# The opening of a fused attention and mixture kernel: the first pair's queries turned in two parts, the second pair's keys turned at once

## The chip, the cores and the metric

The kernel runs on one core of a Trainium2 chip, as one program. The metric is the device time of one execution in microseconds. Three runs of the kernel before took 676.3, 675.15 and 675.15 us; the median is 675.15.

## What is computed

The reference has three parts, and each feeds the next. Only the first matters for the change.

```
B, H, S, D = 4, 8, 576, 64
def rotate(x):                       # by position, halves of D
    x1, x2 = x[..., :32], x[..., 32:]
    return concat([x1*cos - x2*sin, x1*sin + x2*cos])
scores = matmul(rotate(q), rotate(k).T) / sqrt(D)
attn = exp(scores - max(scores));  attn /= sum(attn) + 1e-9
x = matmul(attn, v)                  # 4 x 8 heads of 576 x 64
```

After it come a gated layer with a mixing product over the 576 positions, and four causal attention experts of which each position takes two. All values are float32.

## The kernel before

**Tiling.** The attention goes through the 32 heads as 16 pairs. The two heads of a pair stand one above the other, 64 rows each, in tiles of 128 rows by 576 columns (positions). Queries and keys are loaded together with a copy whose halves are swapped, so that turning (the rotation by position) is three elementwise operations on the whole tile: two multiplications by tables (`rp`) and one sum. Head 1 of a pair has its positions rotated by 64 columns.

**Splitting.** TensorE multiplies at reduced precision, so each turned operand is split: a high part, rounded to `F32R`, and a low part, the remainder. A score tile is a sum of a product of stacked high and low queries (tile `q2`, 128 rows: one head's high part in one half, its low part in the other) with the keys' high part repeated in both halves (`kh`), and a product of the high queries (`qz`, the other half zero) with the keys' low part (`kl`).

**Two ways to fill these operands.** For the first pair of all, `Work.first` (L386 to 416) writes them by engine instructions: ScalarE copies with rounding, VectorE subtracts, GpSimd makes the low parts of columns 256 to 575. For every other pair, `Work.parts` (L426 to 440) makes a high tile `hi` and a low tile `lo`, and `fill_k` (L149) and `fill_q` (L158) spread them by transfers on SyncE's queue: four for the keys, four for the queries (the high part of head 0, its low part, the high part of head 1, its low part).

**The blocks.** A pair has nine score tiles: two heads by four blocks of 128 queries, and one tile of the last 64 of both heads. `slot(k)` (L538) issues one step of the pipeline; with n = k // 9 the pair and x = k % 9 the block, it issues in this order: the exponential of block x (ScalarE), the score products of the next block (TensorE, `scores`), the transposes of the block before (`turn`), the maximum of the next block (VectorE, `maxima`, called the block's maximum here), pending sums of the next pair's turning, the copies of the transposed block, the products with the values, and the preparation of the next pairs. Score tiles alternate between two pairs of banks, so block x + 2 waits for the exponential of block x.

**What sets the order.** All of this is in one program order: `tc.keep_in_program_order` holds for every instruction of an engine (L57 to 61), so each engine runs its own instructions in the order in which the text issues them. A transfer on SyncE's queue that waits holds up those behind it.

**The opening.** L657 to 670 issue what stands ahead of the blocks: 40 products of zeros (`warmed`, two TensorE instructions each), the loads of the first pair in the order keys, tables, queries, constants, values, `first`, the loads of the second pair (keys, then queries), the two multiplications of its keys on GpSimd, its values, the loads of the third pair, the two multiplications of its queries on GpSimd, and then the first score tile and its maximum. Buffers for loaded queries and keys are two deep, so the third pair's loads reuse the first pair's tiles and wait for their last reader. The sums of the second pair follow on VectorE in blocks 2 (keys) and 3 (queries), its parts in blocks 3 (keys) and 4 (queries):

```
            if n == 0 and x in (2, 3):
                works[1].rope(3 - x, (2,), DVE)
...
                if x == (4 if n == 0 else 1):
                    nx.parts(0, DVE if n else ACT)
                if x == (2 if n else 3):
                    nx.parts(1, DVE if n else ACT)
```

Behind each of the first four blocks stand two more zero products (L676). The functions:

Of the kernel before, what the change touches and what calls it, by code (L numbers as in the profile page):

```python
# [12 lines left out]
ALU = mybir.AluOpType  # L13
AX = mybir.AxisListType

B, H, S, D = 4, 8, 576, 64
# [28 lines left out]
def fused_kernel(ctx, tc, qk, v, w_in, w_out, w_sg, g_ln, b_sg, wqk, wvg, wo, rope, cst, out):  # L45
# [68 lines left out]
    class Pair:  # L114
# [43 lines left out]
        def fill_q(self, qh, ql, part=(0, 1)):  # L158
            q2, qz = self.q2, self.qz
            a, c = slice(0, 64), slice(64, 128)  # L160
            todo = [(q2[a, 0, 0:S], qh[a, :]), (qz[a, 0], qh[a, :]), (q2[c, 0, 0:S], ql[a, :])]
            if self.turned:
                def twice(h, o, z, i):
                    o, z, i = f(o), f(z), f(i)
                    o = bass.AP(tensor=o.tensor, offset=o.offset, ap=[o.ap[0], [z.offset - o.offset, 2], [1, S]])
                    return o, bass.AP(tensor=i.tensor, offset=i.offset, ap=[i.ap[0], [0, 2], [1, S]])

                todo = [twice(a, q2[a, 0, 0:S], qz[a, 0], qh[a, :]), (q2[c, 0, 0:S], ql[a, :]),
                        twice(c, q2[c, 1, 64:640], qz[c, 1], qh[c, :]), (q2[a, 1, 64:640], ql[c, :])]
                todo = [x for i, x in enumerate(todo) if i % 2 in part]  # L170
            else:
                todo += [(q2[c, 1, 0:512], qh[c, 0:512]), (qz[c, 1, 64:S], qh[c, 0:512]), (q2[a, 1, 0:512], ql[c, 0:512])]
            if not self.turned:
# [159 lines left out]
    with ExitStack() as st:  # L333
# [30 lines left out]
        class Work:  # L364
# [21 lines left out]
            def first(self):  # L386
# [6 lines left out]
                def low(o, x, h, engine=DVE):  # L393
                    engine.tensor_tensor(o, x, f(h), op=ALU.subtract)

                for t in (k, q):
                    for i in range(2):
                        DVE.tensor_tensor(t[:, i], t[:, i], rp[:, i], op=ALU.mult)
                    DVE.tensor_tensor(t[:, 0], t[:, 0], t[:, 1], op=ALU.add)
                q, k, s, s1 = q[:, 0], k[:, 0], slice(0, S), slice(64, 640)  # L400
                ACT.copy(kh[a, 0], k[a])
                ACT.copy(kh[c, 0], k[a])
                ACT.copy(kh[c, 1], k[c])
                hi = one.tile([P, S], F32R, tag="hi1", name="hi1")
                DVE.tensor_copy(hi, k)
                low(kl, k, hi)
                ACT.copy(kh[a, 1], k[c])
                ACT.copy(q2[a, 0, s], q[a])
                ACT.copy(qz[a, 0], q[a])
                ACT.copy(qz[c, 1], q[c])  # L410
                u, w = slice(0, 256), slice(256, S)
                low(q2[c, 0, u], q[a, u], q2[a, 0, u])
                DVE.tensor_copy(q2[c, 1, s1], q[c])
                low(q2[a, 1, 64:320], q[c, u], q2[c, 1, 64:320])
                low(q2[a, 1, 320:640], q[c, w], q2[c, 1, 320:640], POOL)
                low(q2[c, 0, w], q[a, w], q2[a, 0, w], POOL)

            def rope(self, x, steps=(0, 1, 2), engine=POOL):
                t = self.ts[x]
# [118 lines left out]
        def slot(k):  # L538
# [5 lines left out]

            if w:
                w.exps(x)
            if x == 0 and p:
                p.out(False)
            if x == 4 and p:
# [22 lines left out]
            if x == 0 and p:  # L572
                p.factor(0)

            if n == 0 and x in (2, 3):
                works[1].rope(3 - x, (2,), DVE)
            if wk and not (nx and x == 5):
                if late:
                    wk.place(4)
# [72 lines left out]
        def warmed(n):  # L652

            for _ in range(n):
                PE.matmul(warm[:, 0:P], zero, zero, start=True, stop=True)

        fixed[0] = True  # L657
        warmed(40)
        works[0].load(0)
        works[0].load_values()  # L660
        works[0].first()
        works[1].load(1)
        works[1].rope(1, (0, 1))
        works[1].load_values()
        works[2] = Work()
        works[2].load(2)
        works[1].rope(0, (0, 1))
        works[0].start()
        works[0].scores(0)
        works[0].maxima(0)  # L670
# [2 lines left out]
        for k in range(9 * B * NP + 7):  # L673
            n, x = divmod(k, 9)
            slot(k)
            if k < 4:  # L676
                warmed(2)
            if x in W_AT[4 if n == NP * B - 1 else min(n, 2 + n % 2)]:
# [871 lines left out]
```

## Time and profile before

| | |
|---|---|
| median of three runs | 675.15 us (675.15 to 676.3) |
| profiled execution | 674.28 us, span 672.5 us |
| TensorE busy | 662.9 us, 99% of the span |
| VectorE, ScalarE, GpSimd busy | 446.6, 433.6, 342.3 us |
| granted TensorE clock, mean | 1.000 |

The span is the time from the first to the last instruction of the profiled execution. PE is TensorE, PEld its weight load, DVE VectorE, ACT ScalarE, POOL GpSimd, SPq the queue of SyncE that issues transfers. All engine instructions go through one helper, so the rows carry L59 for nearly everything, and are told apart by their tiles: `ps_S` is a score tile, `ps_t` a transposed one, `ps_l` takes the zero products and small transposes, `ps_o` the products with the values; `t` is the loaded and turned tile, `hi` and `lo` its parts, `q` the operand tile of the queries, `nmax` the maxima, `e` the exponentials. In a timeline, instructions of one kind that follow one another are merged into one row with their count. Ends of TensorE's products are modelled.

### The profile page before, as it was taken

The numbers are of one execution on the slowest core, as the hardware profiler recorded it, in microseconds if no ns is written. First come the engines' busy times: TensorE is split into PE (matmuls) and PEld (weight loads), VectorE is DVE, ScalarE is ACT, GpSimd is POOL, SyncE is SP. The second block draws the span as 40 slices with busy tenths as digits, with TensorE's granted clock in tenths as the row PEclk, the third lists the DMA queues.
The fourth block names the chain that finished last, engine by engine and source line by source line (L and its number), as shares of the span: only waits on it lengthen the run. The fifth ranks groups of instructions, "written<-read, shape, count | busy, mean of one in ns | idle before, by whom it ended". The sixth has DMA issues, their size and how long they took to land.

```text
span 672.5 us, 13535 instructions
## 1 busy us (share of the span) xinstructions
PE 662.9 (99%) x4741; PEld 585.5 (87%) x4741; DVE 446.6 (66%) x1011; ACT 433.6 (64%) x1033; POOL 342.3 (51%) x333
## 2 busy tenths in 40 slices
PE   8999999999999999999999999999999999999997
PEld 8777777777777777798999999999999999999885
DVE  5877777767777776578964764664247666656674
ACT  6777777877878777673563473472146776666774
POOL 2877788888888832642456127206212451542320
PEclk9999999999999999999999999999999999999999
DMA  7798888887888852661374243055466364553522
GB/s 270 209 283 269 249 237 248 242 239 241 228 254 227 249 150 90 182 189 34 118 222 143 89 134 115 12 142 161 121 182 150 92 171 96 135 160 76 143 82 79
DMA packets 64449, 112.83 MB, mean 168 GB/s; under 512 B 18991, under 2 KB 24190, under 8 KB 64382
## 3 DMA queue, kind: packets, MB, share of 16 engines
q1 hardware_dynamic: 61646, 106.29, 54.8%
q10 hardware_dynamic: 2736, 5.68, 2.8%
q8 instruction: 38, 0.62, 0.4%
q14 instruction: 29, 0.24, 0.1%
HBM read 58.06 MB, written 18.98 MB: 115 GB/s over the span
## 4 chain that ended last, share of the span: by engine, by line
PE 87%; DVE 4%; DMA 3%; ACT 2%; issue 1%; POOL 1%; SPq 1%; POOLq 0%; ACTq 0%; DVEq 0%
PE ps_S L59 46%; PE ps_o L59 16%; PE ps_t L59 13%; PE ps_f L59 5%; PE ps_l L59 3%; PE ps_s L59 3%; DMA ws<-in_w_sg_dram 1%; DMA mask<-in_cst_dram 1%; DVE ga L59 1%; DMA q<-lo 0%; DVE nmax L59 0%; DVE t L59 0%; DMA r<-d 0%; DMA sr<-rd 0%; ACT vh L59 0%
## 5 line engine op out<-in xcount | busy, mean ns | idle before, releaser
L59 DVE TENSOR_REDUCE nmax<-ps_S 128x1 f32<-128x576 f32 x144 | 108.8, 756 | 54.3 <-PE ps_S L59 51.6
L59 ACT ACTIVATE e<-ps_S,nmax 128x576 f32<-128x576 f32 x144 | 107.9, 749 | 34.2 <-DVE nmax L59 32.6
L59 PE MATMUL ps_t<-ident,e 128*128 128x128 f32 x776 | 118.1, 273 | 0.0
L59 PEld LDWEIGHTS ps_t<-ident,e 128*128 128x128 f32 x776 | 94.2, 140 | 3.7 <-ACT wih L59 0.4
L59 PE MATMUL ps_S<-kh,q 128*128 128x288 f32 x352 | 84.9, 333 | 2.6 <-ACT e L59 1.4
L59 POOL TENSOR_TENSOR t<-t,rp 128x576 f32<-128x576 f32 x60 | 84.6, 1431 | 0.1
L59 PEld LDWEIGHTS ps_S<-kh,q 128*128 128x128 f32 x352 | 52.2, 189 | 28.8 <-issue 12.8
L59 PE MATMUL ps_o<-g,v 128*64 128x320 f32 (+1 forms) x512 | 72.7, 415 | 0.0
L59 ACT COPY g<-ps_t 128x512 f32<-128x512 f32 x95 | 55.6, 586 | 23.3 <-PE ps_t L59 23.2
L59 POOL TENSOR_TENSOR lo<-t,hi 128x576 fp32r<-128x576 f32 x30 | 43.1, 1438 | 43.6 <-DVE hi L59 42.2
L59 PE MATMUL ps_S<-lo,q 128*128 128x288 f32 x304 | 65.2, 295 | 0.0
L59 PEld LDWEIGHTS ps_o<-g,v 128*64 128x64 f32 x512 | 32.4, 136 | 24.3 <-issue 4.9
L59 PE MATMUL ps_S<-yh,w 128*128 128x288 f32 x256 | 51.8, 304 | 0.0
L59 POOL TENSOR_TENSOR yl<-x,yh 128x640 fp32r<-128x640 f32 (+1 forms) x16 | 25.0, 1564 | 51.6 <-ACT yh L59 51.5
L59 ACT ACTIVATE e<-e,nmax 128x128 f32<-128x128 f32 (+4 forms) x72 | 42.3, 588 | 13.6 <-DVE nmax L59 13.5
L59 PEld LDWEIGHTS ps_S<-lo,q 128*128 128x128 f32 x304 | 48.6, 188 | 0.0
L59 POOL TENSOR_TENSOR t<-t 128x576 f32<-128x576 f32 x28 | 39.7, 1418 | 2.2
L59 ACT ACTIVATE ga<-ga 128x512 f32<-128x512 f32 (+1 forms) x34 | 22.3, 656 | 26.9 <-DVE ga L59 26.9
L59 PEld LDWEIGHTS ps_S<-yh,w 128*128 128x128 f32 x256 | 38.7, 189 | 0.1
L59 POOL TENSOR_TENSOR xl<-sa,xh 128x576 fp32r<-128x576 f32 x12 | 17.7, 1484 | 40.9 <-ACT xh L59 34.7
L59 DVE CUSTOM_DVE_ANT_0 e<-ps_s,mask 128x128 f32<-128x128 f32 (+3 forms) x64 | 31.0, 486 | 7.9 <-PE ps_s L59 6.0
L59 POOL TENSOR_TENSOR gxl<-u,gxh 128x576 fp32r<-128x576 f32 x16 | 22.8, 1429 | 25.3 <-ACT gxh L59 25.3
(283 smaller groups left out, 1758.5 us busy)
## 6 DMA issues: line engine op xcount, KB each, us to landing
t<-in_qk_dram SPq DMA_DIRECT2D x32, 576.0 KB
kh<-hi SPq DMA_DIRECT2D x92, 144.0 KB
q<-hi SPq DMA_DIRECT2D x30, 288.0 KB
q<-lo SPq DMA_DIRECT2D x38, 144.0 KB
v<-in_v_dram SPq DMA_DIRECT2D x16, 320.0 KB
sa<-xr SPq DMA_DIRECT2D x16, 288.0 KB
xd<-sa SPq DMA_DIRECT2D x16, 288.0 KB
xr<-xd SPq DMA_DIRECT2D x16, 288.0 KB
```

Of the source, the lines that this page charges most:

```text
L59: ins = op(*a, **k)
```

## The change

In `first`, the queries' turning is cut at column 320. The function becomes a generator of five steps: the keys and the queries' columns 0 to 319 are turned; then all copies and low parts that these allow, with the queries' copies of head 0 ahead of the second head's keys; behind block 0 the queries' columns 320 to 575 are turned on VectorE; in block 1 their copies and low parts follow (both low parts on GpSimd); in block 2 ScalarE's last copy. The opening has 24 zero products instead of 40. The multiplications of the second pair's keys keep their place in the text, but GpSimd has nothing of `first` ahead of them any more; those of its queries move into block 1, behind the low parts of the first pair's second columns. The sum of the second pair's queries moves from block 3 to block 4. In `fill_q`, when all four transfers are issued together (this is so for the second pair alone), both high parts go ahead of both low parts.

```diff
--- before.py
+++ after.py
@@ -167,7 +167,7 @@
 
                 todo = [twice(a, q2[a, 0, 0:S], qz[a, 0], qh[a, :]), (q2[c, 0, 0:S], ql[a, :]),
                         twice(c, q2[c, 1, 64:640], qz[c, 1], qh[c, :]), (q2[a, 1, 64:640], ql[c, :])]
-                todo = [x for i, x in enumerate(todo) if i % 2 in part]
+                todo = [x for h in part for x in todo[h::2]]
             else:
                 todo += [(q2[c, 1, 0:512], qh[c, 0:512]), (qz[c, 1, 64:S], qh[c, 0:512]), (q2[a, 1, 0:512], ql[c, 0:512])]
             if not self.turned:
@@ -393,27 +393,40 @@
                 def low(o, x, h, engine=DVE):
                     engine.tensor_tensor(o, x, f(h), op=ALU.subtract)
 
-                for t in (k, q):
+                def turn(t, s):
                     for i in range(2):
-                        DVE.tensor_tensor(t[:, i], t[:, i], rp[:, i], op=ALU.mult)
-                    DVE.tensor_tensor(t[:, 0], t[:, 0], t[:, 1], op=ALU.add)
-                q, k, s, s1 = q[:, 0], k[:, 0], slice(0, S), slice(64, 640)
+                        DVE.tensor_tensor(t[:, i, s], t[:, i, s], rp[:, i, s], op=ALU.mult)
+                    DVE.tensor_tensor(t[:, 0, s], t[:, 0, s], t[:, 1, s], op=ALU.add)
+
+                u, w = slice(0, 320), slice(320, S)
+                turn(k, slice(0, S))
+                turn(q, u)
+                yield
+                t, q, k = q, q[:, 0], k[:, 0]
                 ACT.copy(kh[a, 0], k[a])
                 ACT.copy(kh[c, 0], k[a])
+                ACT.copy(q2[a, 0, u], q[a, u])
+                ACT.copy(qz[a, 0, u], q[a, u])
                 ACT.copy(kh[c, 1], k[c])
+                ACT.copy(kh[a, 1], k[c])
+                ACT.copy(qz[c, 1, u], q[c, u])
                 hi = one.tile([P, S], F32R, tag="hi1", name="hi1")
                 DVE.tensor_copy(hi, k)
                 low(kl, k, hi)
-                ACT.copy(kh[a, 1], k[c])
-                ACT.copy(q2[a, 0, s], q[a])
-                ACT.copy(qz[a, 0], q[a])
-                ACT.copy(qz[c, 1], q[c])
-                u, w = slice(0, 256), slice(256, S)
                 low(q2[c, 0, u], q[a, u], q2[a, 0, u])
-                DVE.tensor_copy(q2[c, 1, s1], q[c])
-                low(q2[a, 1, 64:320], q[c, u], q2[c, 1, 64:320])
-                low(q2[a, 1, 320:640], q[c, w], q2[c, 1, 320:640], POOL)
+                DVE.tensor_copy(q2[c, 1, 64:384], q[c, u])
+                low(q2[a, 1, 64:384], q[c, u], q2[c, 1, 64:384])
+                yield
+                turn(t, w)
+                yield
+                ACT.copy(q2[a, 0, w], q[a, w])
+                ACT.copy(qz[a, 0, w], q[a, w])
                 low(q2[c, 0, w], q[a, w], q2[a, 0, w], POOL)
+                DVE.tensor_copy(q2[c, 1, 384:640], q[c, w])
+                low(q2[a, 1, 384:640], q[c, w], q2[c, 1, 384:640], POOL)
+                yield
+                ACT.copy(qz[c, 1, w], q[c, w])
+                yield
 
             def rope(self, x, steps=(0, 1, 2), engine=POOL):
                 t = self.ts[x]
@@ -544,6 +557,10 @@
 
             if w:
                 w.exps(x)
+            if k in (1, 2):
+                next(first)
+            if k == 1:
+                works[1].rope(0, (0, 1))
             if x == 0 and p:
                 p.out(False)
             if x == 4 and p:
@@ -572,8 +589,8 @@
             if x == 0 and p:
                 p.factor(0)
 
-            if n == 0 and x in (2, 3):
-                works[1].rope(3 - x, (2,), DVE)
+            if n == 0 and x in (2, 4):
+                works[1].rope(int(x == 2), (2,), DVE)
             if wk and not (nx and x == 5):
                 if late:
                     wk.place(4)
@@ -655,16 +672,17 @@
                 PE.matmul(warm[:, 0:P], zero, zero, start=True, stop=True)
 
         fixed[0] = True
-        warmed(40)
+        warmed(24)
         works[0].load(0)
         works[0].load_values()
-        works[0].first()
+        first = works[0].first()
+        next(first)
+        next(first)
         works[1].load(1)
         works[1].rope(1, (0, 1))
         works[1].load_values()
         works[2] = Work()
         works[2].load(2)
-        works[1].rope(0, (0, 1))
         works[0].start()
         works[0].scores(0)
         works[0].maxima(0)
@@ -673,6 +691,8 @@
         for k in range(9 * B * NP + 7):
             n, x = divmod(k, 9)
             slot(k)
+            if k == 0:
+                next(first)
             if k < 4:
                 warmed(2)
             if x in W_AT[4 if n == NP * B - 1 else min(n, 2 + n % 2)]:
```

## Rows read from the trace of the kernel before

**Rows 1.** Busy by stretch: us; PE, PEld, DVE, ACT, POOL; clock, DMA share, GB/s
```profile
12.80:30.00 17.20, 14.96 (x116) 12.95 (x115) 12.77 (x20) 12.18 (x29) 15.55 (x12) 1.00 0.65 174
25.00:30.00 5.00, 4.18 (x32) 3.60 (x31) 3.69 (x6) 3.76 (x11) 4.92 (x4) 1.00 0.97 243
30.00:120.00 90.00, 90.00 (x677) 69.67 (x677) 66.08 (x135) 68.84 (x178) 70.07 (x51) 1.00 0.88 260
```

**Rows 2.** Chain of waits, 0 to 60: start us, us, what
```profile
1.04 12.01 PE ps_l L59 x80
...
20.72 1.94 DVE t L59
...
26.07 3.31 DMA q<-lo
```

**Rows 3.** Timeline of TensorE: start us, us, engine, line, operation, [idle before <- releaser]
```profile
15.29 0.53 PE L59 MATMUL ps_S<-kh,q 128*128 128x288 f32 x2 [0.73 <-ACT e L59]
...
24.30 0.53 PE L59 MATMUL ps_S<-kh,q 128*128 128x288 f32 x2
...
27.53 0.50 PE L59 MATMUL ps_S<-kh,q 128*128 128x288 f32 x2 [0.21 <-issue]
...
28.56 0.60 PE L59 MATMUL ps_o<-tl,v 128*128 128x256 f32 x2
29.77 0.50 PE L59 MATMUL ps_S<-kh,q 128*128 128x288 f32 x2 [0.61 <-DMA q<-lo]
```

**Rows 4.** Busy time of TensorE by stretch in the opening, clock, transfers
```profile
2.00:6.00 4.00, 4.00 (x21) 1.00 0.95 323
8.00:12.00 4.00, 4.00 (x39) 1.00 0.93 380
9.00:10.00 1.00, 1.00 (x12) 1.00 1.01 415
```

**Rows 5.** Timeline of VectorE in the opening
```profile
7.08 0.76 DVE L59 TENSOR_TENSOR t<-t 128x576 f32<-128x576 f32 x1
8.04 1.43 DVE L59 TENSOR_TENSOR t<-t,rp 128x576 f32<-128x576 f32 x2 [0.21 <-DMA t<-in_qk_dram]
...
10.18 0.45 DVE L59 CAST hi<-t 128x576 fp32r<-128x576 f32 x1
...
11.46 0.42 DVE L59 TENSOR_TENSOR q<-t,q 64x256 fp32r<-64x256 f32 x1
...
13.62 1.42 DVE L59 TENSOR_REDUCE nmax<-ps_S 128x1 f32<-128x576 f32 x2 [0.80 <-PE ps_S L59]
```

**Rows 6.** Timelines of VectorE and GpSimd, opening and 401 to 406
```profile
20.65 2.00 DVE L59 TENSOR_TENSOR t<-t 128x576 f32<-128x576 f32 x1
...
401.50 0.68 DVE L59 TENSOR_TENSOR vl<-gv,vh 128x512 fp32r<-128x512 f32 x1
402.21 1.80 DVE L59 TENSOR_TENSOR vh<-g,vh 64x512 fp32r<-64x512 f32 x1
...
14.57 6.04 POOL L59 TENSOR_TENSOR t<-t,rp 128x576 f32<-128x576 f32 x4
20.63 1.41 POOL L59 TENSOR_TENSOR lo<-t,hi 128x576 fp32r<-128x576 f32 x1
...
401.84 1.63 POOL L59 TENSOR_TENSOR xl<-sa,xh 128x576 fp32r<-128x576 f32 x1 [0.51 <-ACT xh L59]
403.43 1.88 POOL L59 TENSOR_TENSOR sa<-sa,sr 128x576 f32<-128x576 f32 x1
```

**Rows 7.** Timeline of ScalarE, 22 to 25
```profile
22.68 0.67 ACT L59 CAST hi<-t 128x576 fp32r<-128x576 f32 x1 [0.69 <-DVE t L59]
23.41 0.74 ACT L59 ACTIVATE e<-ps_S,nmax 128x576 f32<-128x576 f32 x1
```

**Rows 8.** Timeline of SyncE's transfer queue, 23 to 26
```profile
23.38 0.64 SPq L178 DMA_DIRECT2D q<-hi  x1
24.88 0.48 SPq L178 DMA_DIRECT2D q<-lo  x1
```

## The prediction

> **What bounds the kernel now.** First the busy time by stretch: from 30.00 to 120.00 TensorE is busy for 90.00 of 90.00 us, from 12.80 to 30.00 for only 14.96 of 17.20 [rows 1]. All that the change edits runs in the first 30 us, and right behind it TensorE has no hole in which a delay could vanish, so a shift of TensorE at 30 us is a shift of the end. What can be gained is bounded too: 2.2 us of holes up to 30, and the stretch ahead of the first scores.
>
> Then the chain of waits in that stretch [rows 2]. It runs through the 80 instructions of the zero products up to 13.05, then through the first scores, and in its second half through the second pair of heads: VectorE's sum for the queries (20.72), ScalarE's copy of it, GpSimd's low part, and the copy transfers, of which the last lands at 26.07 + 3.31 = 29.38. TensorE's own rows end in the same place: it stands 0.61 us until 29.77, where the second pair's second score group begins, and 0.73 until 15.29 [rows 3]. The reader is to see two separate things here: the first scores start when the zero products and the first pair's turning are done, but what sets 29.77 is the second pair's queries.
>
> **The change, part by part.** I follow VectorE, GpSimd and ScalarE in their order of instructions; "before" is the profiled execution.
>
> *Zero products.* 16 fewer are 32 instructions. At the pace of 39 in 4.00 us (8 to 12) they are some 3.5 us, so the block ends at 9.5 and no longer at 13.05 [rows 2, 4]. TensorE is ready then; the scores wait for data.
>
> *Half of the queries first.* The keys' turning is untouched and ends at 7.08 + 0.76 = 7.84. The queries' turning starts at 8.04, as they land [rows 5]. An operation of 320 columns is not shown; 256 columns took 0.42 and 576 took 0.76, so 0.49. Three of them, two overlapping by 0.08, end at 9.46. The copy of the keys (0.45) and their low part (0.76) then end at 10.62. Left alone, the queries' low part, copy and low part (0.49, 0.32, 0.49) would end at 11.9, and the first scores would start at 11.1, not at 12.80.
>
> *GpSimd turns the second pair's keys at once.* They lie behind 960 KB issued after the first queries: constants 64, values 320, the keys' own 576. At 415 GB/s that is 2.37 us from 8.04: they land at 10.4 [rows 4, 5]. From there two multiplications of 1.41 us each run beside VectorE's last four instructions. The trace shows what that costs [rows 6]. A sum on VectorE that began 0.02 us after a GpSimd instruction took 2.00 instead of 0.76, and ended 0.61 after GpSimd's end (22.04). It also shows who goes next: GpSimd came at 401.84 while VectorE's instruction of 401.50 ran; VectorE's next, of 402.21, ended only at 404.01, 0.54 after GpSimd's (403.47); and GpSimd's next ended 1.30 after that. So they take turns, each held for the rest of the other. Applied: the first multiplication comes at 10.41, is held until the keys' low part ends (10.62) and ends at 11.90; the first queries' low part ends at 12.25, the second multiplication at 13.53, the copy at 13.70, the last low part at 14.22. The first scores start at 12.30, 0.5 early, but their maximum stands behind that last low part on VectorE, at 14.14 instead of 13.62. The second scores need it as well: they start at 14.27, and their maximum 0.81 later at 15.08, where before it began at 13.62 + 1.42 - 0.76 = 14.28 [rows 5]. Late by 0.8. Without the collision it would be 1.2 early (13.09, behind ScalarE's last copy at 12.2). I take the collision, since each of the held instructions in rows 6 shows it.
>
> The Trainium skill ("SBUF — State Buffer", "Who interferes with whom") says that the shared pair of ports is locked for a whole instruction, and that a reduction never takes part. The trace agrees with the first: 1.24 us were lost on one sum [rows 6]. By the second the maxima are never held, which leaves the steps above as they are.
>
> *The rest of the queries.* Three operations of 256 columns (0.42) stand behind the second maximum: 15.76 to 16.97. ScalarE's copy of 576 columns took 0.67 [rows 7]; for 256 I take 0.40, so to 17.41. GpSimd, in its order, has idled for this since 13.53. Its two low parts, 256 of 576 columns and so 0.7 instead of 1.41, end at 18.82. Only behind them stand the multiplications of the second pair's queries, held once by the keys' sum on VectorE (18.72 to 19.47): they end at 22.1. Before, all four multiplications were over at 14.57 + 6.04 = 20.61 [rows 6]. GpSimd is 4 us earlier with the keys, which set nothing, and 1.5 us later with the queries, which set the end of the chain.
>
> *The queries' sum, one block later.* As before GpSimd begins its low part of the keys just ahead of it, so the sum ends 0.61 after 23.49, at 24.10, where it ended at 22.65. ScalarE's copy and, behind it in order, the sixth exponential begin at 24.14 and 24.82 (22.68 and 23.41 [rows 7]), and TensorE's eighth score group, which needs the bank that this exponential frees, at 25.70 (24.30 [rows 3]): late by 1.4.
>
> *Order of the query copies.* Both high parts now go ahead of both low ones. Before, the first was issued at 23.38 and the last landed 6.0 us later [rows 2, 8]; from 25 to 30 the transfers were busy for 0.97 at 243 GB/s [rows 1], so the pipe sets this. From 24.84 the last lands at 30.84; the first low part is now third, one transfer of 144 KB (0.6 us) ahead of the last: 30.2. The second pair's first scores need it: they start near 30.15, before at 27.53. The second scores follow 1.3 later (27.53 to 28.56 and one product [rows 3]), at 31.4, where 29.77 stood: +1.6 us. The third pair's queries are loaded later too, at 19.5, since their tile is read up to ScalarE's last copy; 576 KB at 415 GB/s are 1.4 us, and GpSimd asks for them after 26: nothing.
>
> **Sum.** +1.6 us on an execution of 674.28 (span 672.5, 1.8 around it) gives 675.9. That execution lies 0.9 under the median of the runs, so on their scale 676.7.
>
> **Rivals.**
> *The ports don't hold VectorE in the opening* (not slower). Place: VectorE's four instructions between 9.83 and 14.2; it decides at 10.62, where the waiting multiplication gets in or not. For it: three of them work on 64 rows only; against it all of rows 6, where one has 64 rows. The second maximum would begin at 13.09, the rest of the queries be turned by 15.0, the query multiplications end near 19.5, the eighth scores start at 23.0 and the second pair's second scores at 29.0: -0.7 us, 674.4.
> *The copies are not the limit.* The low parts land as early as issue allows, 2.6 us behind 26.3, and the second pair's first scores follow TensorE's own work: 25.70 + 27.53 - 24.30 = 28.9, the second 30.2: +0.4, 675.6. For it: before, the first low part was issued at 24.88, and the first scores began at 27.53; against it the 0.97. The Trainium skill ("DMA: Bandwidth & Descriptors", "Where 436 GB/s comes from") gives 435 GB/s for copies from SBUF to SBUF, by which this rival would hold; the 243 of [rows 1] speaks against it.
> *The clock falls* (slower still). TensorE is empty from 9.5 to 12.3, 2.8 us, four times the longest hole of before. The granted clock reads 1.00 in every row, yet the same product runs 21 times in 4 us at first and 39 times later [rows 4], as at the low level and the high one. At the low level two blocks' work of 3.2 us (24.30 to 27.53) becomes 6.5; one or two blocks cost 0.8 to 3 us more, 678.4.
> *The keys don't start at once*, but after 13 for a wait that the diff doesn't show: then the rest of the queries collides in place of the low parts: +1.4, 676.5.
>
> **How the numbers follow.** The runs shown lie from 675.15 to 676.3, so about 0.2%, 1.35 us, can be told from no change. Chances: the forecast 0.55 (its own range 675.9 to 677.6), free ports 0.12, copies 0.15, clock 0.08, late keys 0.05, anything else 0.05. The forecast sits just above the line at 676.5 and gives 0.35 slower, 0.20 the same; free ports 0.07 the same, 0.05 faster; copies 0.13 the same, 0.02 slower; clock 0.08 slower; late keys half and half; the rest 0.04 faster, 0.01 slower. Together faster 0.09, the same 0.43, slower 0.48. The range runs from 674.4 (free ports) to 678.4 (clock).
>
> **What would show it.** GpSimd's first multiplication at 10.4; VectorE's first queries' low part taking over 1 us from 10.5 on and its copy over 1 us from 12.2 on; the second maximum near 15.1; GpSimd idle from 13.5 to 17.4; the queries' sum ending near 24.1; a TensorE hole of over 1 us ahead of the second pair's first scores near 30.1. Low parts of 0.5 us and a second maximum before 14 would overturn the forecast, and so would second-pair scores before 29.

## The result, and the profile after

The changed kernel takes 681.36 us (median of 6 runs, 679.69 to 687.07), the kernel before 675.12 (6 runs, 673.46 to 676.3): 1.0104 times as long (95% interval 1.0079 to 1.0128). Six more runs on another occasion gave 682.11 against 674.90, 1.0094 (1.0076 to 1.0113). The forecast was 676.7 with a range up to 678.4: slower was right, the size was not. The profiled execution took 679.69, with a span of 677.9 against 672.5; it is the fastest of its six, 1.7 us below their median, so its trace shows less than the whole loss.

| moment, us | before | forecast | after |
|---|---|---|---|
| second maximum begins | 14.29 | 15.08 | 15.83 |
| GpSimd's multiplications of the second pair's queries end | 20.61 | 22.1 | 23.31 |
| their sum ends | 22.65 | 24.10 | 25.31 |
| eighth scores | 24.30 | 25.70 | 26.79 |
| second pair's first scores | 27.53 | 30.15 | 31.66 |
| second pair's second scores | 29.77 | 31.4 | 32.94 |
| last product ends, later than before by | | 1.6 | 5.2 |

Busy time by stretch after, columns as in [rows 1]; the first row is the stretch from the first scores on, with the clock in it:

```profile
11.34:30.00 18.66, 15.27 (x101) 13.38 (x101) 15.42 (x23) 12.15 (x29) 12.71 (x10) 0.83 0.51 139
25.00:30.00 5.00, 3.90 (x33) 3.06 (x27) 3.34 (x7) 3.98 (x10) 3.91 (x3) 1.00 0.78 181
30.00:120.00 90.00, 88.30 (x659) 68.99 (x660) 65.27 (x136) 67.14 (x174) 69.22 (x51) 1.00 0.87 260
```

From 30 to 120 us TensorE now has 1.7 us of holes. TensorE's own stretches (columns of [rows 4]) show a nearly empty engine from 8 to 12 and then the low clock, 0.50, the 1.2 GHz level; by the trace's clock records it stood low from 11.04 to 17.86:

```profile
2.00:6.00 4.00, 4.00 (x29) 1.00 0.95 334
8.00:12.00 4.00, 0.83 (x5) 0.88 0.96 383
12.00:14.00 2.00, 0.67 (x3) 0.50 0.51 136
14.00:18.00 4.00, 3.50 (x16) 0.52 0.21 86
18.00:21.00 3.00, 3.00 (x28) 1.00 0.00 0
```

The zero products ended at 8.17, not at 9.5: the first clock record, the rise to 1.00, lies at 4.21 here and at 6.96 before, and the pace of the products (29 from 2 to 6 us, 21 before) rose with it, though the column reads 1.00 ahead of it too. In zeros24 below, where it rose at 6.88, 24 products end at 9.44. So TensorE stood empty for 3.17 us, until 11.34.

VectorE after (against [rows 5] and [rows 6]):

```profile
10.01 0.76 DVE L59 TENSOR_TENSOR lo<-t,hi 128x576 fp32r<-128x576 f32 x1
10.80 0.48 DVE L59 TENSOR_TENSOR q<-t,q 64x320 fp32r<-64x320 f32 x1
11.32 1.43 DVE L59 CAST q<-t 64x320 fp32r<-64x320 f32 x1
12.78 1.57 DVE L59 TENSOR_TENSOR q<-t,q 64x320 fp32r<-64x320 f32 x1
14.28 0.74 DVE L59 TENSOR_REDUCE nmax<-ps_S 128x1 f32<-128x576 f32 x1
15.83 0.76 DVE L59 TENSOR_REDUCE nmax<-ps_S 128x1 f32<-128x576 f32 x1 [0.81 <-PE ps_S L59]
...
23.35 1.96 DVE L59 TENSOR_TENSOR t<-t 128x576 f32<-128x576 f32 x1 [0.46 <-POOL t L59]
```

and GpSimd beside it:

```profile
10.80 3.20 POOL L59 TENSOR_TENSOR t<-t,rp 128x576 f32<-128x576 f32 x2 [10.36 <-DMA t<-in_qk_dram]
18.41 1.53 POOL L59 TENSOR_TENSOR q<-t,q 64x256 fp32r<-64x256 f32 x2 [4.41 <-issue]
20.02 3.29 POOL L59 TENSOR_TENSOR t<-t,rp 128x576 f32<-128x576 f32 x2
23.27 1.42 POOL L59 TENSOR_TENSOR lo<-t,hi 128x576 fp32r<-128x576 f32 x1
26.09 1.41 POOL L59 TENSOR_TENSOR lo<-t,hi 128x576 fp32r<-128x576 f32 x1 [1.40 <-ACT hi L59]
```

Two VectorE instructions that would take 0.3 to 0.5 last until just behind the end of a GpSimd multiplication (the copy, to 12.75; the last low part, to 14.35). Then GpSimd idles for 4.41 us, does the held-back low parts, and only then the queries of the second pair, 2.7 us later than before. ScalarE follows ([rows 7]), and the transfers ([rows 8], and the piece of the chain of waits that answers to [rows 2]):

```profile
25.34 0.67 ACT L59 CAST hi<-t 128x576 fp32r<-128x576 f32 x1 [1.81 <-DVE t L59]
25.92 0.74 ACT L59 ACTIVATE e<-ps_S,nmax 128x576 f32<-128x576 f32 x1
```

```profile
26.04 1.31 SPq L178 DMA_DIRECT2D q<-hi  x2
27.52 1.82 SPq L178 DMA_DIRECT2D q<-lo  x2
```

```profile
27.52 4.04 DMA q<-lo
```

The copy in this piece is the third of the four, the low part of head 0. By the landing events of the trace the four land at 29.51, 30.89, 31.57 and 32.25 (before, in the old order, at 26.57, 27.43, 28.68 and 29.39).

TensorE after ([rows 3]):

```profile
11.34 0.85 PE L59 MATMUL ps_S<-kh,q 128*128 128x288 f32 x2 [3.17 <-DVE q L59]
...
14.50 0.82 PE L59 MATMUL ps_S<-kh,q 128*128 128x288 f32 x2 [1.83 <-DVE q L59]
...
26.79 0.53 PE L59 MATMUL ps_S<-kh,q 128*128 128x288 f32 x2 [0.91 <-ACT e L59]
...
31.66 0.50 PE L59 MATMUL ps_S<-kh,q 128*128 128x288 f32 x2 [1.84 <-DMA q<-lo]
```

So the opening loses 3.2 us, of which 1.6 were forecast. The other 2 us are lost where the change edits nothing, behind 500 us. SyncE's queue after, and then the same issues in the kernel before:

```profile
494.42 1.87 SPq L262 DMA_DIRECT2D x<-yd  x2
...
543.70 1.70 SPq L188 DMA_DIRECT2D r<-d  x1
```

```profile
491.44 0.88 SPq L262 DMA_DIRECT2D x<-yd  x2
...
539.64 0.59 SPq L188 DMA_DIRECT2D r<-d  x1
```

The first of the two `x<-yd` alone took 1.40 after and 0.40 before. In the packet records of the queue that fetches instructions (q8, 38 packets in either kernel) one packet lies at 494.23 and one at 543.52, right on the two long issues; in the trace of before none lies on these. What follows waits: TensorE's row at 511.80 begins 3.65 us later than its twin before, against 3.15 ahead of it, and the chain of waits to this row runs through the two `x<-yd` issues. At 540.81 it is 4.24: ahead of this row four `kh<-hi` issues from 527.10 on took 2.86 in sum against 2.38, with a third fetch packet (526.88) on them. But the same row comes 0.68 late in lowlater (below) without a longer issue, since a transfer landed later, so the place of this part is less sure. By 553.94, behind the `r<-d` issue, it is 5.2.

### The profile page after: what moved, and what is told of

Same layout as the page of the kernel before. It is cut to its first block, busy times and chain, and to the rows that moved or that the text cites. A ratio compares the mean times of both kernels' runs of the same rounds, so it can differ in the third digit from the quotient of the medians.

```text
span 677.9 us, 13481 instructions
## 1 busy us (share of the span) xinstructions
PE 660.8 (97%) x4709; PEld 582.6 (86%) x4709; DVE 448.4 (66%) x1015; ACT 433.8 (64%) x1036; POOL 342.5 (51%) x333
## 4 chain that ended last, share of the span: by engine, by line
PE 84%; DVE 5%; DMA 5%; ACT 2%; POOL 2%; SPq 1%; issue 1%; ACTq 0%; POOLq 0%
PE ps_S L59 46%; PE ps_o L59 16%; PE ps_t L59 13%; PE ps_f L59 5%; PE ps_s L59 3%; PE ps_l L59 2%; DMA q<-lo 1%; DMA t<-in_qk_dram 1%; DVE t L59 1%; DMA vl<-vst 1%; DVE q L59 1%; DVE e L59 1%; DVE ga L59 0%; POOL t L59 0%; DVE nmax L59 0%
## 5 line engine op out<-in xcount | busy, mean ns | idle before, releaser
L59 POOL TENSOR_TENSOR t<-t,rp 128x576 f32<-128x576 f32 x60 | 85.0, 1438 | 10.4 <-DMA t<-in_qk_dram 10.4
L59 DVE COPY g<-ps_t 128x512 f32<-128x512 f32 x49 | 33.5, 684 | 3.0 <-PE ps_t L59 1.3
```

Of the source, the lines that this page charges most:

```text
L59: ins = op(*a, **k)
```

## The experiments

All comparisons are with the kernel before, run beside each on the same chip; its median was 674.58, 675.41, 674.90, 675.38 and 674.67 in the five groups. "Second scores" is the start of the second pair's second score group (29.77 before, 32.94 after).

**How many products, and how many instructions.** `zeros40` is the changed kernel with 40 products again, `zeros24` the kernel before with 24, `wide24` the kernel before with 24 products that are as long in sum as its 40:

```
 zeros40:  warmed(24) -> warmed(40)                 # in the changed kernel
 zeros24:  warmed(40) -> warmed(24)                 # in the kernel before
 wide24:   warmed(40) -> warmed(24, 213)            # 213 columns each
```

zeros40. 

> The changed kernel with 40 zero products again, nothing else undone. My theory: the changed kernel loses in three places: TensorE's clock (low from 11.0 to 17.9 after a hole of 3.2 us), the second pair's queries that GpSimd multiplies later, and two late transfer issues in the third part. With 40 products the clock stays at 1.00 throughout, the first scores start at 12.8 as before, the second maximum comes at 15.1 to 15.9 (held by GpSimd), the second pair's second scores at 31.2 to 31.8 (29.77 before, 32.94 in the changed kernel): 676.6 to 677.3. Rival A, all of the loss is the clock: 675.1 like before. Rival B, the clock cost nothing, all of it is the order of work: 680 to 681.5.

zeros24. 

> The kernel before with 24 zero products instead of 40, nothing else. My theory: TensorE is empty from 8.2 to 9.5 on until 12.0, so the clock may fall for some 7 us, but what sets 29.8 is the second pair's queries on GpSimd and VectorE, so the opening loses under 1 us; with fewer TensorE instructions the code fetches move against the transfer issues, which can cost 0 to 2 us late: 675 to 677.5. Rival A (all of the loss is the clock): 679 to 681.5. Rival B: 675.1.

wide24. 

> The kernel before, its 40 opening products of 128 zero columns replaced by 24 of 213 (5112 columns in place of 5120): as many TensorE instructions as in the changed kernel, with the work, the clock and the order of before. My theory of the late loss (a transfer issue is held about 1 us when a code fetch falls on it, and which issue that is depends on the number of TensorE instructions ahead): opening as before (29.8), but from 490 to 550 the issues of x<-yd and r<-d take over 1 us and TensorE falls back by 1.5 to 2.5 us there: 676.6 to 677.6. Rival: the late loss comes from the shift of the opening or is chance: 675.1, no late loss.

Measured: zeros40 678.19, 1.0047 (1.0030 to 1.0063), which no expectation held: more than the opening was to cost and less than the changed kernel; zeros24 676.88, 1.0029 (1.0014 to 1.0044), and wide24 676.69, 1.0031 (1.0016 to 1.0046), both where the theory had them. In zeros40 the second scores begin at 32.66, and another hole opens far behind the opening, ahead of the scores of a later pair; oldorder (below), with the same order of instructions, has it too:

```profile
205.50 0.50 PE L59 MATMUL ps_S<-kh,q 128*128 128x288 f32 x2 [1.23 <-DMA xr<-xt]
```

wide24 keeps the clock at 1.00 and the start of TensorE's work as it was (first scores 12.87, before 12.80), and still loses as much as zeros24; 0.9 us of what its profiled execution loses is its opening (second scores 30.66), where the tables landed 0.9 later. What it shares with zeros24 is that TensorE has 64 instructions fewer (two products and two weight loads for each of the 16). Its `x<-yd` issue is long at the same place:

```profile
493.04 2.67 SPq L262 DMA_DIRECT2D x<-yd  x2
```

**Place of the code in the changed kernel.** `afterwide` gives the changed kernel 24 products of 213 columns, `aftertiny` puts 16 products of 4 columns ahead of its 24, and `tiny16` does that in the kernel before; `after2` is the changed kernel again.

after2. 

> The changed kernel once more, beside the kernels of this group: 680.3 to 681.6 by every theory; its ratio to before is what the others are compared with.

afterwide. 

> The changed kernel whose 24 zero products are 213 columns wide: TensorE's number of instructions is the changed kernel's, its opening is as busy as with 40 products. Theory A (placement of code: fetches fall on issues of transfers, some 2 us behind 180 us of the run): 679.8 to 681.0. Rival B (what the changed kernel lost beyond its 40-product version is the stretch of low clock behind the short row of products): 678.0 to 678.8.

aftertiny. 

> The changed kernel with 16 zero products of 4 columns ahead of its 24: TensorE has as many instructions as before again, while the work of the opening and its clock stay nearly as in the changed kernel. Theory A, placement: the changed kernel has 64 instructions of TensorE fewer, so the fetches of code fall on other issues of transfers than before; this gives back what the kernel before lost by 24 wider products, 1.5 to 2.5 us: 678.3 to 679.6. Rival B, clock: the loss beyond 678.2 (40 products) is that of TensorE's 6.8 us at the low clock, which stays: 680.5 to 681.5.

tiny16. 

> The kernel before with 16 zero products of 4 columns and 24 of 128 in place of 40 of 128: the number of TensorE instructions of before, the work of 24 products, so that TensorE stands idle for some 3 us before the first scores. Theory A, placement: no late issues, and the idle stretch costs nothing that lasts: 674.5 to 675.6, where 24 products alone gave 676.9. Rival B, clock: the idle stretch lowers the clock from 13.7 us on and that is the 2.3 us that 24 products cost: 676.4 to 677.3.

Measured: after2 682.11, 1.0094; afterwide 680.15, 1.0080 (1.0059 to 1.0101), in the placement's range and not in the clock's, though its profiled opening was at the low clock too, from 14.16 to 17.57; aftertiny 678.91, 1.0058 (1.0043 to 1.0073), inside the placement's range too, though its clock also stayed up once it was granted. tiny16 missed: 676.87, 1.0028 (1.0018 to 1.0038). Its trace says why, in TensorE's rows:

```profile
1.05 15.07 PE L59 MATMUL ps_l<-zero 128*128 128x4 f32 x80 [1.05 <-DVE zero L59]
15.88 0.51 PE L59 MATMUL ps_S<-kh,q 128*128 128x288 f32 x2
```

The clock rose only at 13.39 (6.96 before), so the products ended 3 us late and the second scores began at 32.79. From there to the end this version lost nothing more (-0.1 us): the loss is its own opening, and the run doesn't test the clock after the products.

Over all traces the place of the code shows best in how much the shift against before grows from 480 us to the end. In the five with 24 products it is 2.2, 2.4, 2.0, 1.6 and 1.9 us; in the fourteen with the old number of instructions it lies between 0.0 and 1.4, but for keysonly (below) with 2.4. In all five the same `x<-yd` issue takes 1.32 to 2.19 us; in the kernel before and in all fourteen it takes 0.40. Counted in TensorE's own instructions (products and weight loads), the fetch of 16 KB behind 480 us lies at the 7069th to 7078th in these fifteen and at the 7091st to 7094th in the five, whatever its time, so it goes with TensorE's stream. The number of instructions is not the only way to it: in keysonly, whose opening is late and whose TensorE has the old number, a fetch packet (507.49) lies on another `x<-yd` issue, which took 0.58 before:

```profile
507.29 1.76 SPq L262 DMA_DIRECT2D x<-yd  x1
```

**GpSimd's order and the collision.** `keyshold` (zeros40, with GpSimd's keys held behind VectorE's last low part by a one-column copy), `qfirst` (zeros40, with the second pair's queries multiplied right behind the keys), `keysonly` (the kernel before with one part of the change, the keys at once):

```
 keyshold:  + POOL.tensor_copy(gate[a], f(q2[a, 1, 64:65]))      # behind the last low part
 qfirst:    works[1].rope(1, (0, 1)); + works[1].rope(0, (0, 1)) # taken out of slot 1
 keysonly:  works[1].load(1); works[1].rope(1, (0, 1)); works[0].first()
```

keyshold. 

> The changed kernel with 40 zero products, and GpSimd's multiplications of the second pair's keys held behind VectorE's last low part of the first pair (by a copy of one column on GpSimd that reads it), so that nothing of GpSimd runs beside VectorE's opening. If the ports cost VectorE the opening: its last low part ends at 11.9 to 12.2 (14.35 in the changed kernel), the second maximum starts at 14.3 (15.83), and everything behind, the second pair's second scores too, comes 0.6 to 1.2 us earlier than in the version with 40 zero products alone. If the ports cost nothing: the same times as that version.

qfirst. 

> The changed kernel with 40 zero products at its start, and GpSimd multiplies the second pair's queries right behind its keys, ahead of the first pair's held-back low parts. Theory A: what makes the opening late is that GpSimd's multiplications of the second pair's queries stand behind low parts that wait for VectorE's second turn (they ended at 22.96 in the run with 40 zero products, at 20.61 before); here they end at 17.0 to 17.8, the sum starts with its slot at 21 to 22 instead of 23.65, and the second pair's second scores begin at 30.6 to 31.4 instead of 32.66: 676.2 to 677.0. Rival B: the first pair's low parts, now 0.7 to 1.5 us later, hold TensorE at the fifth scores by as much as is gained: 677.8 to 678.6. Rival C: the loss is that of the clock's low stretch alone, no order on GpSimd matters: 678.0 to 678.4.

keysonly. 

> The kernel before with one part of the change alone: GpSimd multiplies the second pair's keys as soon as they land, ahead of the first pair's low parts. Theory A: VectorE's low parts and casts from 10.7 us on are stretched by about 2 us, the first scores begin 0.5 to 2 us later, but GpSimd's multiplications of the second pair's queries end 1.0 to 1.8 us earlier than before (20.61), since GpSimd no longer idles until 12.45; TensorE's holes before 30 us take the delay: 674.0 to 675.3, no difference or a small gain. Rival: the collision costs what it cost the changed kernel, its 1 to 2 us stay at the second pair's first scores: 676.0 to 676.8.

Measured: keyshold 677.67, 1.0042 (1.0030 to 1.0055); qfirst 678.83, 1.0064 (1.0046 to 1.0081); keysonly 677.33, 1.0031 (1.0012 to 1.0049). In keyshold the collision is gone from VectorE's low parts:

```profile
11.38 0.48 DVE L59 TENSOR_TENSOR q<-t,q 64x320 fp32r<-64x320 f32 x1
11.90 0.33 DVE L59 CAST q<-t 64x320 fp32r<-64x320 f32 x1
12.26 0.49 DVE L59 TENSOR_TENSOR q<-t,q 64x320 fp32r<-64x320 f32 x1
...
14.49 1.95 DVE L59 TENSOR_TENSOR t<-t,rp 128x256 f32<-128x256 f32 x2
```

The last line shows that it was moved rather than removed: GpSimd's keys now run from 13.03 to 15.81, and the turning of the second columns beside them takes 1.95 where it took 0.76 after the change. The second scores come 0.7 us earlier than in zeros40 (31.97, 32.66), as expected, but in time it is 0.3 to 0.5 and the intervals overlap: GpSimd still waits for the held-back columns (its low parts begin at 17.46, its multiplications end at 22.2). qfirst failed: GpSimd runs 6.08 us without a gap and holds a third VectorE instruction (13.79, 1.57 us), the second maximum moves to 16.47, and the sum of the queries, which stands in its block, begins at 23.80 although its inputs were ready at 16.6. keysonly: one part of the change alone costs 2.1 us by the ratio (0.8 to 3.3), in the rival's range. Its trace can't say why: the profiled execution is the slowest of twelve (681.4), at the low clock from 14.16 to 20.99, and its second scores at 33.09 hold that too, while GpSimd's multiplications of the queries ended earlier than before (19.52), as the theory had it.

**The order of the copies.** `oldorder` and `qboth` put the line in `fill_q` back, in zeros40 and in qfirst; `heldorder` binds the order high, low, high, low in zeros40; `orderonly` binds high, high, low, low in the kernel before.

```
 heldorder, orderonly:  + with tc.issue_after(d.ins): d = nc.sync.dma_start(f(o), f(i))
```

oldorder. 

> The changed kernel with 40 zero products at its start and, of the change, all but the order of the copies of the second pair's queries: high, low, high, low as before, in place of high, high, low, low. In the run with 40 zero products and the rest of the change, the second pair's second scores began 2.9 us later than before (32.66 against 29.77), its median 678.2. Theory A: in the changed order the last low part lands before the pair's first scores, whose 1.3 us of TensorE work then stand behind the last landing instead of ahead of it; with the old order the first scores begin by 29.7 and the second right behind the last landing, at 31.5 to 31.9, so 0.8 to 1.1 us earlier: 677.1 to 677.4. Rival: the four copies share one queue, so that the order among them changes nothing: second scores at 32.5 to 32.8, 678.0 to 678.4.

qboth. 

> The last two edits together: 40 zero products, the second pair's queries multiplied right behind its keys, and the copies in the order of before. Theory A: both gains add, second scores at 29.8 to 30.5: 675.2 to 676.1, within 1.5 us of the kernel before; what is left is the clock's low stretch and VectorE's held low part. Rival: the copies move one behind the other at some 225 GB/s and end no earlier than 30.6 us whatever starts them, second scores at 31.2 or later: 676.6 to 677.4.

heldorder. 

> The changed kernel with 40 zero products, where the second pair's four copies of queries are bound to the order high, low, high, low that the trace of before shows (the edit tried before did not change the order of issue: it was high, high, low, low still). Theory A: the first scores of the second pair no longer wait for the last copy; they begin by 30.0 and the second ones at 31.5 to 32.0 instead of 32.5 to 32.7: 677.2 to 677.8. Rival: the last copy lands no earlier and later than 31 us, the second scores stay at 32.4 to 33.1: 678.0 to 678.8.

orderonly. 

> The kernel before, with the second pair's four copies of queries bound to the order that the changed kernel takes: high, high, low, low in place of high, low, high, low. Theory A (the order is a part of the loss by itself, as holding the old order in the changed kernel gave 1.4 us back): the pair's first scores wait for the third or fourth copy and begin at 28.8 to 29.8 instead of 27.53, the second at 30.4 to 31.1 instead of 29.77: 675.6 to 676.4. Rival: in the kernel before the last copy lands at the same moment in either order and TensorE has work until then: 674.6 to 675.2.

The line alone changed nothing: every engine's order in oldorder is that of zeros40, and qboth's copies go as qfirst's, so these two tested no order and are repeats. The helper that keeps the program order wraps four engines and not SyncE's transfers, so the new order of the copies is not the doing of the line in `fill_q`; which part of the change turns it was not tested. The repeats took 678.36, 1.0043 (1.0030 to 1.0056), and 678.94, 1.0053 (1.0036 to 1.0069). One thing they give: in oldorder's profiled opening the clock, once it had risen, stayed at 1.00, that of zeros40 had it at 0.50 from 15.60 to 19.02, and their second scores are 32.49 and 32.66. heldorder took 676.78, 1.0029 (1.0018 to 1.0039), by the ratios 1.0 to 1.2 us less than the two versions without the binding; the intervals just overlap. In its trace the first scores follow the second copy, which lands at 30.11; in zeros40 they wait for the third, which lands at 31.29, not for the last, as the expectation of oldorder has it:

```profile
30.20 0.50 PE L59 MATMUL ps_S<-kh,q 128*128 128x288 f32 x2
...
32.48 0.51 PE L59 MATMUL ps_S<-kh,q 128*128 128x288 f32 x2 [0.65 <-DMA q<-lo]
```

The second ones moved by only 0.2, not by the 0.5 to 1.2 expected, though the first copy was issued 0.4 later than in zeros40. From the issue of the first copy to the second scores it takes 6.4 to 6.6 us in nine of the ten traces with the old order (allheld, below, 7.0) and 6.8 to 7.0 in nine of the ten with the new one (after2 8.2): in the traces the order costs some 0.4 us. orderonly took 675.59, 1.0010 (1.0000 to 1.0021): first scores 1.5 later, second ones 0.5, a cost at the edge of what can be told.

**Both together, and VectorE instead of GpSimd.** `heldkeys` is keyshold with the order held (`heldkeys2` the same again); `allheld` moves in addition the held-back low parts to VectorE and the queries up on GpSimd.

heldkeys. 

> The changed kernel with 40 zero products, the old order of the second pair's copies held, and GpSimd's multiplications of the keys held behind VectorE's last low part, so that the two engines do not collide. Theory A (collision and order are separate terms): the order gives 1.4 us back as it did with the collision, the hold some 0.5 more: 675.8 to 676.5, second scores at 30.6 to 31.3. Rival B (the collision is no term, GpSimd's late low parts of the held-back columns are all that is left): 676.5 to 677.1, as with the order alone (676.8).

heldkeys2. 

> The changed kernel with 40 zero products, the old order of copies held and GpSimd's keys held behind VectorE's last low part, once more: its twelve times lay between 675.4 and 683.4, although the opening of its profile was the earliest of all versions. Theory A (two separate terms): 675.8 to 676.8, and the late times before were chance. Rival (something behind the opening, which the one profile didn't show, costs this version 2 us in most executions): 677.8 to 679.

allheld. 

> The last kernel, and in it VectorE, not GpSimd, takes the low parts of the held-back columns, and GpSimd multiplies the second pair's queries right behind the keys. Theory A (all that is lost in the opening is collision, copies' order and GpSimd's wait for the held-back columns): GpSimd's multiplications end by 19.5 (20.61 before), the sum of the queries by 22.3 (22.65), second scores at 29.3 to 30.2: 674.2 to 675.4, level with before. Rival B (turning the columns in two parts costs by itself, on VectorE and in the slots that follow): 676.0 to 677.0.

Measured: heldkeys 678.51, 1.0044 (1.0023 to 1.0065), with times from 675.43 to 683.42, and 677.09, 1.0039 (1.0027 to 1.0051); its openings are the earliest of the changed ones (31.52, 31.43), yet its time is no lower than heldorder's. The collision is neither shown nor excluded as a term of its own: as in keyshold, it met the turning of the second columns instead (1.94 and 1.32 for the two multiplications, 0.76 after the change). allheld is the worst of these, 680.79, 1.0095 (1.0070 to 1.0119). VectorE, and under it GpSimd:

```profile
12.57 1.43 DVE L59 TENSOR_REDUCE nmax<-ps_S 128x1 f32<-128x576 f32 x2 [0.29 <-PE ps_S L59]
14.03 3.15 DVE L59 TENSOR_TENSOR t<-t,rp 128x256 f32<-128x256 f32 x2
17.21 1.50 DVE L59 TENSOR_TENSOR t<-t 128x256 f32<-128x256 f32 x1
```

```profile
12.56 5.87 POOL L59 TENSOR_TENSOR t<-t,rp 128x576 f32<-128x576 f32 x4
```

The rest of the turn takes 4.7 us where it took 1.2 after the change (16.62 to 17.83): the collision was moved, not removed, and each of the three instructions pays about one GpSimd instruction. The two maxima beside the same GpSimd run take what they always take.

**Taking the collision away in the kernel before.** `lowlater` exchanges two GpSimd instructions of the kernel before: the keys' low part goes behind the queries'.

lowlater. 

> The kernel before, of the change nothing, with one pair of GpSimd instructions exchanged: the low part of the second pair's keys stands behind that of its queries, so that GpSimd is idle while VectorE adds the queries (that sum took 2.00 us beside the keys' low part; 0.75 to 0.77 where GpSimd was idle, in the runs with the collision moved away). Theory A (each VectorE instruction that meets a GpSimd one waits for its end, and this wait is on the path that ends in the second scores): the sum ends 0.9 to 1.2 us earlier, the queries' copies are issued 0.6 to 0.9 us earlier, the second pair's second scores begin at 28.9 to 29.4 instead of 29.77: 674.0 to 674.8 beside 674.9 to 675.4 for before, a gain at the edge of what can be told. Rival (the four copies of the keys fill the transfer engines until 24 us and set the last landing): second scores at 29.6 or later, no difference.

Measured: 673.98 against 674.67, 0.9992 (0.9983 to 1.0002). The sum that took 2.00 [rows 6] is free of GpSimd, whose next instruction comes later:

```profile
21.34 0.75 DVE L59 TENSOR_TENSOR t<-t 128x576 f32<-128x576 f32 x1
```

```profile
23.35 2.79 POOL L59 TENSOR_TENSOR lo<-t,hi 128x576 fp32r<-128x576 f32 x2 [2.05 <-ACT hi L59]
```

The second scores begin at 29.68, in an execution whose tables landed 0.8 us later than in the one before. The sum ended 0.55 earlier, but the first copy was issued at 23.32, hardly ahead of before (23.38), not 0.6 to 0.9 earlier; in its place of the second scores the rival was right. It is the only version with a median below the kernel before; the interval includes no change.

## Why the prediction was wrong

- *What bounds the kernel.* Right about the opening: the chain after runs through the same sum, low part and copy. The sentence "a shift of TensorE at 30 us is a shift of the end" is the first step that failed. The shift was 3.2 at 32.94 and 5.2 at the end. wide24 shows that fewer TensorE instructions cost some 2 us by themselves, 2.1 by its ratio; afterwide agrees, its 1.0080 lies 2.2 to 2.5 us above the 1.0047 and 1.0043 of the versions with 40, though the ends of the intervals touch (1.0059 and 1.0063). The sentence fails with the old number of instructions too: holes open ahead of later pairs, 1.23 us at 205.50 in zeros40 and 1.78 at 78.08 in orderonly. *Zero products* were counted as time on TensorE only; that they also set where in TensorE's stream its code is fetched was no term and no rival.
- *Half of the queries, keys at once.* Right in kind: GpSimd's first multiplication at 10.80 (10.4 forecast), first scores early (11.34), the copy and the last low part held until a GpSimd instruction ended. The low part at 10.80 got in first; the second maximum came 0.75 later than forecast. Of that 0.23 is the later start of the second scores (14.50 for 14.27); the rest is that they took 1.33 us until the maximum in place of 0.81, at the low clock. In zeros40, whose clock was high until 15.60, they took 0.81 (14.66 to 15.47).
- *The rest of the queries* is the mis-sized term of the opening. Forecast was 1.5 us for GpSimd's multiplications of the queries, measured 2.7: the low parts began at 18.41 instead of 17.41, 0.75 of it inherited from the maximum, and ran 0.1 longer. Everything behind kept the forecast's distances: sum +1.45 forecast and +2.66 measured, eighth scores +1.4 and +2.5.
- *Order of the copies.* Right in kind: the first scores (31.66) followed the third copy (31.57), the last landed 0.7 behind it, 6.2 us after the first issue (6.0 forecast), and the second scores came 1.3 behind the first. From the first issue to the second scores it was 6.90 us, 6.56 forecast and 6.39 before, so the order was priced 0.3 too low; the other 1.2 of the opening's error is the step above. The order came about, but not by the line in `fill_q` that the forecast read it from: that was luck. Binding the old order gave 1.0 to 1.2 us back by time, 0.4 to 0.6 by the traces.
- *Rivals.* Free ports, copies that are no limit and late keys are refuted by the same rows. "The clock falls", held at 0.08 with one or two blocks at the low level, did happen, and in the profiled opening it cost less than the 0.8 to 3 us priced: after with 6.8 us at the low clock and afterwide with 3.4 reach the second scores at 32.94 and 32.95, since the blocks there wait for GpSimd. In other executions it may cost more: after2 was low again from 33.03 to 36.44, where TensorE has no holes, and its second scores began at 35.52. The mean clock of every execution is on record. Among the 164 of the changed kernel and the variants, those with a lower clock took longer than others of the same kernel: 0.63 us for each 0.001 (standard error 0.08), some 1.6 us for a stretch of 3.4 us at the low level. That is no proof of a cause, since an opening that is late for another reason leaves holes too, and it does not hold everywhere: zeros40's six runs lie at 0.997, five of oldorder's six at 0.999 or 1.000, at ratios of 1.0047 and 1.0043. The changed kernel's twelve lie at 0.990 to 0.995. Between the changed kernel (1.0104, 1.0094) and afterwide (1.0080) lie 1 to 1.6 us, but their intervals overlap.
- *Sum.* By medians: 3.0 to 3.6 us for the change with 40 products (forecast 1.6), of which the order of the copies is 0.4 to 1.2 and, in the profiled executions, about 1 a hole far behind the opening; 2.1 to 2.5 for the place of the code; up to 1.6 left for the idle stretch and its clock. How the rest of the opening divides between the collision and GpSimd's wait for the held-back columns stays open: keysonly, without held-back columns, costs 2.1, heldkeys and heldkeys2, with the keys held, 3.0 and 2.6, and no run has the held-back columns without a collision.

## What to carry to other kernels

An idle engine is no free place for work: before moving an instruction to GpSimd, list the VectorE instructions that read and write SBUF beside it, also where you hold it back, and what stands behind it in GpSimd's order. When a change adds or removes instructions on any engine, look far behind the edit for transfer issues that became long. Differences of under 1 us in one profiled opening did not show reliably in medians here; only a change's time over several runs, with an interval, decides. Look where the profiled execution lies among them: keysonly's was the slowest of twelve, the changed kernel's the fastest of six.

## What was not expected of the hardware

- Some issues on SyncE's queue on which an instruction fetch lies took 0.9 to 1.8 us longer than without it (0.40 became 1.32 to 2.19, 0.59 became 1.70). The `x<-yd` issue behind 490 us was long in all five traces with 64 TensorE instructions fewer, wide24's with its longer products among them, and in none of the fifteen others. Behind 30 us 274 issues of the 20 traces took over 0.3 us longer than the median of the same issue; a fetch packet lies on 255 of them, though most issues that touch one (1018 of 1273) are not longer.
- With the same loads ahead, VectorE's multiplication by the second half of the rotation tables began between 6.05 (orderonly) and 7.31 us (keyshold); in two executions of the same changed kernel it was 6.12 and 7.29: more than a microsecond of scatter at the start.
- With sixteen products of 4 columns ahead of 24 of 128 the clock rose at 13.39 in one execution and at 11.40 in another; in the other 18 profiled executions it rose between 3.90 and 7.02.
- VectorE and GpSimd took turns one instruction at a time whatever VectorE's size (64 x 320 or 128 x 256), while two reductions from PSUM ran beside GpSimd in 1.43, as without it [rows 5]. The Trainium skill ("SBUF — State Buffer", "Who interferes with whom") says that a lock on a shared pair of ports is the only contention of the two. The rows agree as far as they go: VectorE's instructions were held beside GpSimd's (allheld) and not where GpSimd was idle (lowlater).
